# One long stretch of each matmul kind per block, with two of eight ReLUs on VectorE: a fused dynamic convolution and feed-forward kernel on one Trainium2 core

## Chip, cores, metric

The kernel runs on one core of one Trainium2 (trn2) chip. The metric is device time in microseconds (us), lower is better. All runs that are compared here are in the same (fast) state. The kernel before took 791.85 us (790.45 to 792.14).

## The reference, cut to what matters

```python
# x (8, 4096, 192), weight_gen (8, 4096, 8 heads, 7 taps), w_in (192, 2048), w_out (2048, 192)
w = softmax(weight_gen, axis=-1)                # per token and head, 7 taps
x_pad = concatenate([zeros(B, 6, D), x], axis=1)
y[b, s, h, :] = sum_k w[b, s, h, k] * x_pad[b, s + k, h, :]      # causal dynamic convolution
y = y.reshape(32768, 192)
out = maximum(y @ w_in, 0) ** 2 @ w_out         # squared-ReLU feed-forward, fp32 out
```

## The kernel before

Tokens are handled in 64 blocks of 512, eight to a batch. For each block TensorE does three things: the convolution (`yp`, as small matmuls against banded weights `bd`), MM1 (`h = y @ w_in`, 96 matmuls of 64 rows x 256 columns, twelve to each of eight "pairs" of 128-wide chunks of the 2048 hidden features) and MM2 (`o = g @ w_out`, 64 matmuls of 192 columns). Between MM1 and MM2, ScalarE takes the ReLU out of PSUM (`t`), and VectorE squares it (`g`). The softmax of the next batch is spread over the blocks: its exp is on ScalarE, the rest on VectorE. Its result goes to DRAM (`vd`) and comes back as rows (`wr`), from which VectorE makes the bands.

```python
    p_t1 = ctx.enter_context(tc.tile_pool(name="p_t1", bufs=5))
    ps_h = ctx.enter_context(tc.tile_pool(name="ps_h", bufs=3, space=bass.MemoryType.PSUM))  # 128x1024 fp32 each: yp and h
    ps_o = ctx.enter_context(tc.tile_pool(name="ps_o", bufs=1, space=bass.MemoryType.PSUM))  # 2 tiles of 128x512 fp32: o
    # ... cut ...
    def st_relu(j, fp):
        t1 = p_t1.tile([P, 2, 2, TH], f16, name="t1")
        t1_t[(j, fp)] = t1
        nc.scalar.activation(out=t1, in_=h_t[(j, fp)], func=ActF.Relu)

    def st_sq(j, fp):
        g = p_g.tile([P, 2, 2, TH], f16, name="g")
        g_t[(j, fp)] = g
        t1 = t1_t[(j, fp)]
        nc.vector.tensor_tensor(out=g, in0=t1, in1=t1, op=AluOp.mult)
    # ... cut ...
    G0, G1 = (0, 1, 2, 3), (4, 5, 6, 7)
    # ... cut: the start, until the loop over blocks ...
        for j in range(NBLK):
            # ... cut: weight_gen and x loads ...
            late = j == 2
            if j:
                if j + 1 < NBLK:
                    st_conv_alloc(j + 1)
                    st_conv(j + 1)
                    st_y_evac(j + 1)
                if not late:
                    st_bands(j + 2, 0)
            for fp in G0:
                st_mm1(j, fp)
                st_relu(j, fp)
                st_sq(j, fp)
            if j:
                for half in (0, 1):
                    st_mm2(j - 1, G1, (half,))
                    o_copy(j - 1, half, nc.scalar.copy)
                o_store(j - 1, (0, 1), nc.sync)
            # ... cut: block 0 ...
            if not late:
                st_bands(j + 2, 1)
            if hi and j:
                s = rows_of[nb]
                softmax(s, lo, hi)                 # exp on ScalarE, sum, reciprocal, scale on VectorE
                if hi == s.rh:
                    s.store(nc.sync)
            for fp in G1:
                st_mm1(j, fp)
                st_relu(j, fp)
                st_sq(j, fp)
            st_mm2(j, G0)
            # ... cut ...
            if j + 3 < NBLK:
                wr_load(j + 3)
```

MM1 and MM2 thus come in four stretches a block, of four pairs each.

The softmax here doesn't subtract the row's maximum and nothing guards it: scores larger than these inputs give would overflow.

Of the kernel before, what the change touches and what calls it, by code (L numbers as in the profile page):

```python
# [9 lines left out]
def kernel(  # L10
# [20 lines left out]
    nc = tc.nc  # L31
    f32 = mybir.dt.float32
    f16 = mybir.dt.float16
# [8 lines left out]
    P = 128  # L42
    TB = 512
    NBB = S // TB
    NBLK = B * NBB
    NF = Dff // P
    NFP = NF // 2
# [3 lines left out]
    HALO = KK - 1  # L51
    SL = 8
    TH = TB // 2
# [19 lines left out]
    p_wr = ctx.enter_context(tc.tile_pool(name="p_wr", bufs=4))  # L73
    p_bd = ctx.enter_context(tc.tile_pool(name="p_bd", bufs=3))
    p_y = ctx.enter_context(tc.tile_pool(name="p_y", bufs=2))
    p_t1 = ctx.enter_context(tc.tile_pool(name="p_t1", bufs=5))
    p_g = ctx.enter_context(tc.tile_pool(name="p_g", bufs=10))
    p_os = ctx.enter_context(tc.tile_pool(name="p_os", bufs=2))
    p_dr = ctx.enter_context(tc.tile_pool(name="p_dr", bufs=3, space=bass.MemoryType.DRAM))
# [30 lines left out]
    def load_w_in(q):  # L110
        c = slice(q * NQ, (q + 1) * NQ)
        w_sa[q] = p_st.tile([P, NQ], f32, name="w_sa")
        w_sb[q] = p_st.tile([RT, NQ], f32, name="w_sb")
        nc.sync.dma_start(out=w_sa[q], in_=moe_w_in[0:P, c])
        nc.sync.dma_start(out=w_sb[q], in_=moe_w_in[P:D, c])  # L115
# [136 lines left out]
    def x_load(j):  # L252
        x_t[j] = p_x.tile([P, NT, D], f16, name="xt")
        block_load(j, x_t[j], x[j // NBB], D, nc.gpsimd)
# [11 lines left out]
        wr = wr_t[j].rearrange("p t g c -> p t (g c)")  # L266
        block_load(j, wr, vd_t[j // NBB], H * SL, nc.sync)

    def wr_load_sbuf(j, s, order, engines):

        wr_t[j] = p_wr.tile([P, NT, HP, SL * 2], f16, name="wr")
        for n, i in enumerate(order):
            t0 = max(j * TB + tile_start(j, i), 0)
            engines[n % len(engines)].dma_start(
                out=wr_t[j][:, i].rearrange("p g c -> p (g c)"),
                in_=s.v[t0 // s.r : (t0 + P) // s.r, HALO : HALO + s.r].rearrange(
                    "p r g c e -> p r (g c e)"
                ),
            )

    def st_band(j, tiles):

# [88 lines left out]

    def st_mm2(j, fps, halves=(0, 1)):

        if fps[0] == 0:
            o_t[j] = [ps_o.tile([P, TB], f32, name=f"o{half}") for half in range(2)]
        o = o_t[j]
        for fp in fps:
            for jj in range(2):
                fc = 2 * fp + jj
                for half in halves:  # L380
                    for cc in range(2):
                        nc.tensor.matmul(  # L382
                            out=o[half][:, cc * Dm : (cc + 1) * Dm],
                            lhsT=g_t[(j, fp)][:, half, jj, cc * P : (cc + 1) * P],
                            rhs=w_o[:, fc, :],
                            start=(fc == 0 and cc == 0), stop=(fc == NF - 1),
                            skip_group_check=True,
                        )

    def st_relu(j, fp):  # L390
        t1 = p_t1.tile([P, 2, 2, TH], f16, name="t1")
        t1_t[(j, fp)] = t1
        nc.scalar.activation(out=t1, in_=h_t[(j, fp)], func=ActF.Relu)  # L393

    def st_sq(j, fp):
        g = p_g.tile([P, 2, 2, TH], f16, name="g")
        g_t[(j, fp)] = g
        t1 = t1_t[(j, fp)]
        nc.vector.tensor_tensor(out=g, in0=t1, in1=t1, op=AluOp.mult)  # L399

    def o_copy(j, half, copy):
        if half == 0:
# [17 lines left out]
            for tiles in (groups, ((NT - 1,),))[part]:  # L420
                st_band(j, tiles)

    G0, G1 = (0, 1, 2, 3), (4, 5, 6, 7)
    UNIT = 4

    with nc.allow_low_precision("fp16 matmul pipeline"), tc.manual_schedule():

        vd0 = new_vd(0)
        parts = [
            Softmax(0, P * sum(FIRST[:i]), r, v_first[i], vd0) for i, r in enumerate(FIRST)  # L430
        ]
        warm = const.tile([P, TB], f16, name="warm")
        nc.vector.memset(warm, 0.0)  # L433
        for i in (0, 1):
            nc.vector.memset(v_first[i], 0.0)

        wp = ps_h.tile([P, 2 * TB], f32, name="wp", tag="h")

        def spin(n):
            for i in range(n):  # L440
                nc.tensor.matmul(  # L441
                    out=wp[:, 0:TB], lhsT=warm[:, 0:P], rhs=warm, start=True, stop=True
                )

        def softmax(s, lo, hi):
            s.exp(lo, hi)
            s.recip(lo, hi)
            s.scale(lo, hi, nc.vector)

        vec, act, pool = nc.vector.tensor_copy, nc.scalar.copy, nc.gpsimd.tensor_copy  # L450
        s0, s1, s2 = parts
        spin(36)
        band_mask()
        s0.load(nc.sync)
        load_w_in(0)
        load_w_in(1)
        x_load_f32(0)
        s0.exp(0, s0.rh)
        s0.recip(0, s0.rh)
        s0.scale(0, s0.rh, nc.vector)  # L460
        cast_w_in(0, "straight", act)
        cast_w_in(0, "up", act)
        cast_w_in(0, "down", pool)
        cast_w_in(0, "last", act)
        cast_w_in(0, "last up", act)
        wr_load_sbuf(0, s0, (0, 1, 2, 4, 3), (nc.sync, nc.gpsimd))
        cast_w_in(1, "up", vec)
        cast_w_in(1, "down", vec)
        x_load(1)
        s1.load(nc.sync)  # L470
        for q in range(4):
            load_w_out(q, 4)
        nc.gpsimd.memset(v_first[2], 0.0)
        x_cast(0, act)
        wr_load_sbuf(1, s0, range(NT), (nc.sync,))
        s0.store(nc.sync)
        s2.load(nc.sync)
        cast_w_in(1, "straight", act)
        cast_w_in(1, "last", act)
        for i in (0, 2, 1, 3, 4):  # L480
            st_band(0, (i,))
        st_conv_alloc(0)
        st_conv(0)
        spin(4)
        s1.exp(0, s1.rh)
        st_y_evac(0)
        cast_w_in(1, "last up", act)
        x_load(2)
        nc.gpsimd.memset(v_big, 0.0)
        st_bands(1, 0)  # L490
        st_bands(1, 1)
        s1.recip(0, s1.rh)
        s1.scale(0, s1.rh, nc.vector)
        s1.store(nc.sync)
        wr_load(2)


        plan = {}

        def spread(b, rh, blocks):  # L500
            lo = 0
            for n, j in enumerate(blocks):
                left = len(blocks) - n
                hi = min(lo + -(-(rh - lo) // (UNIT * left)) * UNIT, rh)
                if lo < hi:
                    plan[j] = (b, lo, hi)
                lo = hi

        spread(0, s2.rh, (0, 1))
        for b in range(1, B):  # L510
            first = NBB * (b - 1)
            spread(b, R + HALO, range(first + (2 if b == 1 else -2), first + 5))
        rows_of = {0: s2}

        for j in range(NBLK):
            nb, lo, hi = plan.get(j, (None, 0, 0))
            after = plan.get(j + 1)
            if after and after[1] == 0:
                s = Softmax(after[0], 0, R, v_big, new_vd(after[0]))
                s.load(nc.sync)  # L520
                rows_of[after[0]] = s
            if j + 3 < NBLK:
                x_load(j + 3)

            late = j == 2
            if j:
                if j + 1 < NBLK:
                    st_conv_alloc(j + 1)
                    st_conv(j + 1)
                    st_y_evac(j + 1)  # L530
                if not late:
                    st_bands(j + 2, 0)
            for fp in G0:
                st_mm1(j, fp)
                st_relu(j, fp)
                st_sq(j, fp)
            if j:
                for half in (0, 1):
                    st_mm2(j - 1, G1, (half,))
                    o_copy(j - 1, half, nc.scalar.copy)  # L540
                o_store(j - 1, (0, 1), nc.sync)
            elif NBLK > 1:
                st_conv_alloc(1)
                st_conv(1)
                st_y_evac(1)
                st_bands(2, 0)
            if not late:
                st_bands(j + 2, 1)
            if hi and j:
                s = rows_of[nb]  # L550
                softmax(s, lo, hi)
                if hi == s.rh:
                    s.store(nc.sync)
            for fp in G1:
                st_mm1(j, fp)
                st_relu(j, fp)
                st_sq(j, fp)
            st_mm2(j, G0)
            if hi and not j:
                softmax(rows_of[nb], lo, hi)  # L560
            if late:
                st_bands(j + 2, 0)
                st_bands(j + 2, 1)
            if j + 3 < NBLK:
                wr_load(j + 3)
        st_mm2(NBLK - 1, G1, (0,))
        o_copy(NBLK - 1, 0, nc.scalar.copy)
        st_mm2(NBLK - 1, G1, (1,))
        o_store(NBLK - 1, (0,), nc.sync)
        o_copy(NBLK - 1, 1, nc.vector.tensor_copy)  # L570
        o_store(NBLK - 1, (1,), nc.scalar)
# [30 lines left out]
```

## Time and profile before

| | before |
|---|---|
| time, median of three runs | 791.85 us |
| span of the profiled execution, granted clock | 789.8 us, 0.991 |
| busy: TensorE, ScalarE, VectorE | 98%, 77%, 74% |
| share of TensorE in the chain that ended last | 94% |

The granted clock is the mean share of TensorE's full clock that the chip granted. The prediction below shows the lines; in them PE is TensorE, PEld its weight loads, DVE VectorE, ACT ScalarE, POOL GpSimd, SP SyncE, and L363 is line 363 of the kernel. A page of the profile is read here in this order: busy shares, the chain that ended last (what the end of the program hung on), the costliest groups, then the timeline of one ordinary block. One caution is needed throughout. Matmul records overlap and their ends are modelled (a 64x256 matmul is recorded with 269 ns, though the next pair starts after 109), so a wait of up to some 0.16 us between two matmuls does not appear as idle time at all. I therefore also made a **ledger**: TensorE's stream from the first MM1 on is cut into stretches of one kind; a stretch lasts from its first matmul's start to the next stretch's first; what it lasts beyond the shortest of its kind is waiting. As the shortest I take 2.726 us for 48 matmuls of MM1, 2.745 for 32 of MM2, 0.84 for a convolution, and 5.345 and 5.384 for the long stretches of MM1 and MM2.

For before the ledger is: first MM1 at 19.0 us, 753.2 us of stretches at their shortest, 13.6 us of waits, 4.0 us from the last matmul to the end.

### The profile page before, as it was taken

How to read it: one execution, taken by the hardware profiler on the slowest of the kernel's cores; microseconds unless marked ns; L12 is line 12 of the kernel's file. 1: busy time of each engine (PE TensorE's matmuls, PEld its weight loads, DVE VectorE, ACT ScalarE, POOL GpSimd, SP SyncE). 2: the span in 40 equal slices, each digit the busy share in tenths (PEclk: the TensorE clock that was granted, in tenths of full speed). 3: DMA queues.
4: the chain of work that ended last, by engine and by line, in shares of the span. 5: the costliest groups of instructions: out<-in, count | busy, mean ns of one | idle time of the engine just before them, and what ended most of it. 6: DMA issues, size and time to landing. Idle time of an engine off the chain costs nothing.

```text
span 789.8 us, 32661 instructions
## 1 busy us (share of the span) xinstructions
PE 774.0 (98%) x14888; PEld 680.1 (86%) x14888; DVE 584.0 (74%) x1042; ACT 610.7 (77%) x761; POOL 73.6 (9%) x96
## 2 busy tenths in 40 slices
PE   7889999999999999999999999999999999999997
PEld 3777888888888888888888888888888888889887
DVE  5787778777877768877777767877688777666653
ACT  6776777877887787787787787787787787787785
POOL 7101000010001000010001000011000010000000
PEclk8998999999999999999999999999999999999999
DMA  9832533336333443336333363333533344342111
GB/s 212 169 76 43 152 53 68 70 53 149 72 53 65 106 106 63 69 59 146 67 61 62 68 146 63 64 64 63 145 69 59 63 71 80 67 73 43 51 41 41
DMA packets 123929, 64.09 MB, mean 81 GB/s; under 512 B 87281, under 2 KB 121104, under 8 KB 123024
## 3 DMA queue, kind: packets, MB, share of 16 engines
q1 hardware_dynamic: 79744, 45.51, 20.8%
q0 software_dynamic: 43776, 16.31, 19.5%
q8 instruction: 116, 1.90, 1.0%
q14 instruction: 21, 0.17, 0.1%
q10 hardware_dynamic: 272, 0.20, 0.1%
HBM read 48.74 MB, written 29.36 MB: 99 GB/s over the span
## 4 chain that ended last, share of the span: by engine, by line
PE 94%; DMA 3%; DVE 2%; SPq 0%; ACT 0%; issue 0%; DVEq 0%
PE o L382 44%; PE h L363 44%; PE yp L338 7%; DMA x_st<-in_x_dram 1%; DMA wr<-v_first 1%; DVE bd L289 1%; DMA vd<-v_first 1%; DMA wr<-vd 0%; DVE g L399 0%; DVE ssum L180 0%; DVE rcp L185 0%; DVE v_big L193 0%; DVE v_first L193 0%; ACT ex L172 0%; SPq L115 0%
## 5 line engine op out<-in xcount | busy, mean ns | idle before, releaser
L393 ACT ACTIVATE t<-h 128x1024 f16<-128x1024 f32 x512 | 483.0, 1030 | 9.7 <-PE h L363 9.2
L399 DVE TENSOR_TENSOR g<-t 128x1024 f16<-128x1024 f16 x512 | 344.9, 690 | 144.5 <-ACT t L393 144.0
L363 PE MATMUL h<-y,w_i 64*128 64x256 f16 x6144 | 363.7, 271 | 0.7 <-ACT t L393 0.3
L382 PE MATMUL o<-w_o,g 128*128 128x192 f16 x4096 | 360.0, 246 | 0.0
L382 PEld LDWEIGHTS <-g 128*128 128x128 f16 x4096 | 331.5, 98 | 26.8 <-DVE g L399 16.7
L363 PEld LDWEIGHTS <-w_i 64*128 64x128 f16 x6144 | 293.0, 94 | 50.5 <-issue 12.8
L289 DVE TENSOR_TENSOR bd<-wr,mask 128x1664 f16<-128x1664 f16 (+2 forms) x201 | 160.8, 832 | 15.4 <-DMA wr<-vd 12.6
L351 ACT CAST y<-yp 128x768 f16<-128x768 f32 x64 | 51.2, 799 | 119.2 <-PE yp L338 119.2
L250 POOL DMA_DIRECT2D xt<-in_x_dram x63 | 52.2, 830 | 472.3 <-PE yp L338 448.4
L404 ACT COPY o_sb<-o 128x384 f32<-128x384 f32 x127 | 62.8, 495 | 38.2 <-PE o L382 38.2
L338 PE MATMUL yp<-bd,xt 128*32 128x104 f16 (+12 forms) x4608 | 60.4, 204 | 10.0 <-DVE bd L289 6.1
L338 PEld LDWEIGHTS <-xt 128*32 128x32 f16 (+3 forms) x4608 | 51.4, 91 | 21.1 <-issue 16.7
L180 DVE TENSOR_REDUCE ssum<-ex 128x64 f32<-128x448 f32 (+6 forms) x49 | 25.9, 529 | 32.9 <-ACT ex L172 32.9
L193 DVE TENSOR_TENSOR v_big<-ex,rcp 128x112 f16<-128x112 f32 (+3 forms) x192 | 32.8, 235 | 1.6
L172 ACT ACTIVATE ex<-wg 128x448 f32<-128x448 f32 (+6 forms) x49 | 26.5, 542 | 1.8 <-DMA wg<-in_weight_gen_dram 1.8
L185 DVE RECIPROCAL rcp<-ssum 128x64 f32<-128x64 f32 (+6 forms) x49 | 23.3, 476 | 1.7
L244 POOL DMA_DIRECT2D xt<-in_x_dram x10 | 5.7, 569 | 86.9 <-PE yp L338 86.9
L441 PE MATMUL wp<-warm 128*128 128x512 f16 x40 | 11.4, 450 | 1.3 <-DVE warm L433 1.3
L240 POOL DMA_DIRECT2D xt<-in_x_dram x7 | 3.8, 543 | 78.0 <-PE yp L338 78.0
L441 PEld LDWEIGHTS <-warm 128*128 128x128 f16 x40 | 4.3, 111 | 7.1 <-issue 2.8
L193 DVE TENSOR_TENSOR v_first<-ex,rcp 128x112 f16<-128x112 f32 (+2 forms) x32 | 6.0, 258 | 0.2
L127 ACT CAST w_i<-w_sa 128x1024 f16<-128x1024 f32 (+1 forms) x3 | 3.1, 1043 | 1.4 <-DMA w_sa<-in_moe_w_in_dram 1.4
(19 smaller groups left out, 22.9 us busy)
## 6 DMA issues: line engine op xcount, KB each, us to landing
out_dram<-o_sb SPq DMA_DIRECT2D x63, 384.0 KB, 2.8
xt<-in_x_dram POOLq DMA_DIRECT2D x46, 240.0 KB, 4.3
wg<-in_weight_gen_dram SPq DMA_DIRECT2D x6, 1064.0 KB, 5.8
wr<-vd SPq DMA_DIRECT2D x46, 80.0 KB, 3.0
vd<-v_big SPq DMA_DIRECT2D x7, 512.0 KB, 3.5
xt<-in_x_dram POOLq DMA_DIRECT2D x17, 192.0 KB, 3.9
w_sa<-in_moe_w_in_dram SPq DMA_DIRECT2D x2, 512.0 KB, 6.7
wr<-vd SPq DMA_DIRECT2D x16, 64.0 KB, 2.8
```

The costliest lines, as they stand in the source:

```text
L172: nc.scalar.activation(out=self.ex[:, lo:hi].rearrange("p r g k e -> p (r g) k e"), in_=self.wg[:, lo:hi].rearrange("p r (g e) k -> p (r g ...
L180: nc.vector.tensor_reduce(out=ssum.rearrange("p r g e -> p (r g) e"), in_=self.ex[:, lo:hi].rearrange("p r g k e -> p (r g) e k"), axis=Ax ...
L193: eng.tensor_tensor(out=bass.AP(tensor=v.tensor, offset=v.offset + lo * H * SL + lo % SL * 2 + g * SL * 2, ap=[list(v.ap[0]), [H * SL + 2, ...
L250: eng.dma_start(out=dst[:, first:last], in_=ap)
L289: nc.vector.tensor_tensor(out=bd_t[j][:, H * lo : H * hi].rearrange("p (g m c) -> p g m c", g=shape[1], c=2 * SL), in0=wr_t[j][:, i : tile ...
L338: nc.tensor.matmul(out=yp_t[j][p0 : p0 + m, col + a : col + b], lhsT=x_t[j][:, i, 32 * q : 32 * q + m], rhs=bd[:, h // 2, h % 2, a - lo : ...
L351: nc.scalar.copy(out=y, in_=yp_t[j][:, 0 : NK * TH].rearrange("p (k c) -> p k c", k=NK))
L363: nc.tensor.matmul(out=h[:, half, jj, :], lhsT=w_i[r0 : r0 + RT, slot, fc * P : (fc + 1) * P], rhs=y_t[j][r0 : r0 + RT, k, :], start=(jj = ...
L382: nc.tensor.matmul(out=o[half][:, cc * Dm : (cc + 1) * Dm], lhsT=g_t[(j, fp)][:, half, jj, cc * P : (cc + 1) * P], rhs=w_o[:, fc, :], star ...
L393: nc.scalar.activation(out=t1, in_=h_t[(j, fp)], func=ActF.Relu)
L399: nc.vector.tensor_tensor(out=g, in0=t1, in1=t1, op=AluOp.mult)
L404: copy(out=o_sb_t[j][:, half], in_=o_t[j][half][:, 0 : 2 * Dm])
```

## The change

The intent: fewer changes between matmul kinds. All eight pairs of a block go through MM1 in one stretch, then through MM2 in one. ScalarE alone could not drain eight pairs at MM1's pace (0.904 us a pair against 0.655, worked out in the prediction), so VectorE takes the ReLU of pairs 1 and 4, and ScalarE their squares. The bands of block j+2 stay ahead of MM1 in program order. The requests for the rows of block j+3 go ahead of the output store. At the start (where `spin` issues matmuls on a tile of zeros named `warm`), x is loaded ahead of the second half of `w_in`, the second softmax part later, and block 2 takes its rows from SBUF. The core of the diff, cuts marked:

```diff
-    p_t1 = ctx.enter_context(tc.tile_pool(name="p_t1", bufs=5))
+    p_t1 = ctx.enter_context(tc.tile_pool(name="p_t1", bufs=6))
+    p_t1s = ctx.enter_context(tc.tile_pool(name="p_t1s", bufs=2))
 ... cut ...
     def st_relu(j, fp):
-        t1 = p_t1.tile([P, 2, 2, TH], f16, name="t1")
+        swapped = fp in swapped_of(j)
+        t1 = (p_t1s if swapped else p_t1).tile([P, 2, 2, TH], f16, name="t1")
         t1_t[(j, fp)] = t1
-        nc.scalar.activation(out=t1, in_=h_t[(j, fp)], func=ActF.Relu)
+        if swapped:
+            nc.vector.tensor_scalar_max(out=t1, in0=h_t[(j, fp)], scalar1=0.0)
+        else:
+            nc.scalar.activation(out=t1, in_=h_t[(j, fp)], func=ActF.Relu)
 ... cut: st_sq, with ScalarE's Square for swapped pairs ...
-    G0, G1 = (0, 1, 2, 3), (4, 5, 6, 7)
+    SWAPPED = (1, 4)
+    SQ_AT = {3: (0,), 7: (2, 3, 5, 6, 7)}
+    MM2 = (0, 2, 3, 5, 6, 7, 1, 4)
 ... cut: the start ...
-        spin(36)
+        spin(42)
         load_w_in(0)
-        load_w_in(1)
         x_load_f32(0)
 ...
+        load_w_in(1)
         x_load(1)
+        wr_load_sbuf(1, [s0], range(NT), (nc.sync,))
         s1.load(nc.sync)
 ... cut: the loop ...
                 if not late:
                     st_bands(j + 2, 0)
-            for fp in G0:
+            for fp in range(NFP):
                 st_mm1(j, fp)
                 st_relu(j, fp)
-                st_sq(j, fp)
-            if j:
-                for half in (0, 1):
-                    st_mm2(j - 1, G1, (half,))
-                    o_copy(j - 1, half, nc.scalar.copy)
-                o_store(j - 1, (0, 1), nc.sync)
+                if not j:
+                    st_sq(j, fp)
+                    if fp == 1:
+                        rest_of_s1()
+                elif fp in SQ_AT:
+                    for sq in SQ_AT[fp]:
+                        st_sq(j, sq)
 ... cut ...
-            if hi and j:
+            if hi:
                 s = rows_of[nb]
                 softmax(s, lo, hi)
                 if hi == s.rh:
                     s.store(nc.sync)
-            for fp in G1: ...
-            st_mm2(j, G0)
             if j + 3 < NBLK:
                 wr_load(j + 3)
+            for fp in swapped_of(j):
+                st_sq(j, fp)
+            st_mm2(j, MM2[:4])
+            for half in (0, 1):
+                st_mm2(j, MM2[4:], (half,))
+                if more or half == 0:
+                    o_copy(j, half, nc.scalar.copy)
+            if more:
+                o_store(j, (0, 1), nc.sync)
```

## The prediction

> **What bounds the kernel now.** I read the busy shares first, then the chain that ended last, then the costliest groups. The page says:
>
> ```profile
> PE 774.0 (98%) x14888; PEld 680.1 (86%) x14888; DVE 584.0 (74%) x1042; ACT 610.7 (77%) x761; POOL 73.6 (9%) x96
> ...
> PE 94%; DMA 3%; DVE 2%; SPq 0%; ACT 0%; issue 0%; DVEq 0%
> PE o L382 44%; PE h L363 44%; PE yp L338 7%; DMA x_st<-in_x_dram 1%; DMA wr<-v_first 1%; DVE bd L289 1%; DMA vd<-v_first 1%; DMA wr<-vd 0%; DVE g L399 0%; DVE ssum L180 0%; DVE rcp L185 0%; DVE v_big L193 0%; DVE v_first L193 0%; ACT ex L172 0%; SPq L115 0%
> ```
>
> TensorE carries 94% of the chain: L382 (MM2), L363 (MM1), L338 (convolution). ScalarE and VectorE are a quarter idle, so only what changes TensorE's own stream, or makes it wait, counts. The timeline of one undisturbed block (columns: start, us, engine, line, tile, count) shows that stream:
>
> ```profile
> 406.23 0.90 PE L338 MATMUL yp<-bd,xt 128*32 128x104 f16 x72
> ...
> 407.06 2.79 PE L363 MATMUL h<-y,w_i 64*128 64x256 f16 x48
> ...
> 409.79 2.81 PE L382 MATMUL o<-w_o,g 128*128 128x192 f16 x32
> ...
> 412.53 2.90 PE L363 MATMUL h<-y,w_i 64*128 64x256 f16 x48
> ...
> 415.37 2.81 PE L382 MATMUL o<-w_o,g 128*128 128x192 f16 x32
> ...
> 418.11 0.91 PE L338 MATMUL yp<-bd,xt 128*32 128x104 f16 x72
> ```
>
> A block takes 418.11 - 406.23 = 11.88 us, in five stretches with no gap of note. The start times of single matmul records refine this: inside MM1 two matmuls start per 109 ns (54.5 each), inside MM2 one per 82.5 ns. So 48 x 54.5 = 2.62 us, yet the next stretch begins 2.73 us after this one; 32 x 82.5 = 2.64, yet 2.74 pass. **Each change of stretch costs about 0.105 us** (95 ns before the first matmul of the new kind, 10 ns after it).
>
> [...] MM1 is 64*128, MM2 128*128[...]. [...] the last output copy,
>
> ```profile
> L404 DVE COPY o_sb<-o 128x384 f32<-128x384 f32 x1 | 0.6, 558 | 2.8 <-PE o L382 2.8
> ```
>
> [...] After the early wait shown below an MM1 stretch takes 4.78 us instead of 2.79[...].
>
> **The change, part by part.**
>
> (a) Switches. Now a block has conv, MM1, MM2, MM1, MM2: five changes. Afterwards conv, MM1, MM2: three. Two fewer x 0.105 us x about 63 blocks = **-13 us**. Eighteen blocks also have an MM1 stretch of 2.83 us instead of 2.73, because ScalarE does the softmax's exp just before it (the 2.90 line above is one). That is another -2 us.
>
> (b) Work moved. Two of eight ReLUs go from ScalarE to VectorE, their squares go the other way. A VectorE ReLU on 128x1024 fp32 in PSUM is, from the 558 ns row, [...] **about 1.22 us** (estimate). In heavy blocks VectorE then does 2 x 1.22 + 6 x 0.61 + band products 1.95 + 0.55 + softmax 2.0 = 10.6 us of about 12: tight, but no bound. ScalarE keeps some 10 us (evacuation 0.80, six ReLUs 5.4, two squares about 1.9, two copies 1.0, exp 0.62).
>
> (c) New waits in MM1. This is where I differ from the intent. The rows used:
>
> ```profile
> L393 ACT ACTIVATE t<-h 128x1024 f16<-128x1024 f32 x512 | 483.0, 1030 | 9.7 <-PE h L363 9.2
> L399 DVE TENSOR_TENSOR g<-t 128x1024 f16<-128x1024 f16 x512 | 344.9, 690 | 144.5 <-ACT t L393 144.0
> L351 ACT CAST y<-yp 128x768 f16<-128x768 f32 x64 | 51.2, 799 | 119.2 <-PE yp L338 119.2
> ```
>
> TensorE fills a pair of h in 12 x 54.5 = 0.655 us. ScalarE needs 1.03 us, or 0.904 from start to start when queued. There are three h buffers. Four pairs just fit today: in single records the fourth pair starts 80 ns after its buffer's ReLU ended. Eight in a row do not. I walk it with t = 0 at the start of MM1, a ReLU startable 0.216 us after its pair's matmuls are issued, and 0.05 us from a ReLU's end to the next matmul in that buffer (both seen in single records). Buffers rotate: A = yp, h2, h5; B = h0, h3, h6; C = h1, h4, h7.
> - ReLU1 on VectorE: 1.32 + 0.216 = 1.54 to 2.76. h4 wants C at 2.63 and gets it at 2.81: **0.18 us lost**.
> - ReLU0 0.87 to 1.90; ReLU2 from 2.19; ReLU3 is queued behind it, 3.09 to 4.13. h6 wants B at 4.12, gets it at 4.18: **0.06 lost**.
> - ReLU4 on VectorE 3.68 to 4.90. h7 wants C at 4.83, gets it at 4.95: **0.12 lost**.
>
> Sum 0.36 us per block, against the 0.21 saved: **+0.15 us per block**. Even with an instant VectorE the h0-h3-h6 chain on ScalarE alone costs 4.18 - 3.94 = 0.24 us, so the switches' saving is then merely cancelled.
>
> (d) A new wait in MM2. Squares 1 and 4 stand behind the exp on ScalarE. ReLU7 ends near 7.17; exp of 0.62 to 7.67; the squares, 1.03 each as from this row's neighbour L393, end near 8.6 and 9.5. MM2 starts at 5.7 and wants pair 4, last of the first half, at 5.7 + 44 x 0.0825 = 9.35. Loss about 0.25 in blocks with the 0.62 us exp (18 of them), where (a) returned 0.1, and little in the others.
>
> The mean over a batch of eight blocks is about +0.21 us per block; x 62 = **+13 us** net, everything in (a) to (d) included.
>
> (e) The start. Before, it has three losses in the timeline:
>
> ```profile
> 13.60 0.99 ACT L262 CAST xt<-x_st 128x960 f16<-128x960 f32 x1 [3.11 <-DMA x_st<-in_x_dram]
> ...
> 30.38 2.43 DVE L289 TENSOR_TENSOR bd<-wr,mask 128x1664 f16<-128x1664 f16 x3 [4.51 <-DMA wr<-vd]
> ...
> 59.50 0.27 PE L338 MATMUL yp<-bd,xt 128*32 128x104 f16 x2 [2.74 <-DVE bd L289]
> ...
> 61.74 4.78 PE L363 MATMUL h<-y,w_i 64*128 64x256 f16 x48
> ```
>
> Fetching x before the second half of w_in takes 0.79 MB out of its way: at the 200 GB/s reached then, x lands nearer 10 us, and I give the first MM1 2 to 3 us. The rows of block 2 come from SBUF instead of by a store and reload (TensorE lost about 2.6 us there). The bands of block 4 move ahead of MM2, removing the 2.7 us wait and the slow clock after it (2.0 us). Against this: VectorE now has bands ahead of ReLU1. In block 1 those wait for rows stored late (I put some 1.7 us); in block 3 the large first softmax (1.09 + 0.95 + 1.58 in block 2) delays them by about 2 us. Also the second half of w_in, cast by GpSimd at 1.03 us a piece, may come late. Net **about -6 us**.
>
> (f) Row loads ahead of the output store only reorder two transfers that land in 3 us and are needed a block later: 0.
>
> Sum: 791.85 + 13 - 6 = about 798.
>
> **Rivals.** *The change works as meant*: no new waits, -13 -2 -6 gives 771. For it: VectorE's slack, and order lists tuned by someone with a purpose. Against: three buffers, and the 80 ns margin of today. It needs h buffers to come free earlier than any row here says. *VectorE becomes the bound*: if its ReLU takes 1.35 us, MM1 waits grow to about 0.6 us per block, and with the bands ahead of ReLU1 late in heavy blocks the time is 815 or more. For it: 10.6 us of 12, in strict order. Against: after the softmax and the next bands VectorE is free at about 12.2, and ReLU1 is wanted at 13.6. *The start alone moves*: steady waits just cancel the switches (the 0.24 us floor), giving 786 to 790.
>
> **Range and chances.** An error of 0.1 us in the steady block is 6 us, and the start is uncertain by 4. So 780 to 813. Faster than 776 needs nearly every wait of (c) absent: 0.09. Slower than 807.7 needs 0.15 us per block more than worked out, or a bad start: 0.17. Within 2%: 0.74.
>
> **What would show it.** Changes of stretch near 0.105 us, three per block: (a). VectorE's ReLU row near 1220 ns: (b). "PE h" waiting for t of VectorE at the fifth and eighth pair, for t of ScalarE at the seventh, 0.3 to 0.4 us per block: (c). MM2 waiting for ScalarE's g in blocks with the long exp: (d). First MM1 near 16 to 17 us, no loss near 59 us, a wait for VectorE in blocks 1 and 3: (e). A steady block near 11.93 us without exp and 12.2 with the long one. The prediction is wrong if MM1 of a steady block runs in 5.34 us without waits, or if VectorE is late for ReLU1 in every block.

## The result, and the profile after

The changed kernel took **826.24 us** (median of 4 runs, 824.39 to 827.1); before, in the same rounds, 792.0 us. The ratio is 1.043 (95% interval 1.0403 to 1.0457). The change made the kernel 4.3% slower, outside the predicted range of 780 to 813 us.

The page of the changed kernel, its busy shares and the chain that ended last:

```profile
PE 788.7 (96%) x14894; PEld 704.2 (85%) x14894; DVE 624.9 (76%) x1040; ACT 631.5 (77%) x759; POOL 78.3 (9%) x100
...
PE 67%; ACT 10%; DVE 10%; DMA 6%; issue 4%; SPq 2%; ACTq 0%; DVEq 0%
```

The busy shares hardly tell anything: 96 instead of 98%. The chain does: TensorE carried 94% of it, and now 67%; ScalarE, VectorE and DMA have entered it. The costliest groups on the two drain engines (count, busy us, mean ns of one, idle before):

```profile
L407 ACT ACTIVATE t<-h 128x1024 f16<-128x1024 f32 x386 | 374.3, 1023 | 52.4 <-PE h L369 52.4
...
L405 DVE TENSOR_SCALAR t<-h 128x1024 f16<-128x1024 f32 x126 | 154.3, 1224 | 143.6 <-PE h L369 140.0
...
L295 DVE TENSOR_TENSOR bd<-wr,mask 128x1664 f16<-128x1664 f16 (+2 forms) x201 | 160.8, 837 | 41.4 <-DMA wr<-vd 31.2
...
L414 ACT ACTIVATE g<-t 128x1024 f16<-128x1024 f16 x126 | 126.8, 1067 | 0.0
```

VectorE's ReLU takes 1224 ns, close to the estimate of 1.22 us, which can be worked out from the trace of before: 558 ns for 384 elements a partition (the output copy), and 640 more at 1.04 ns each (its softmax sums, `ssum`, take 967 ns for 784 elements and 386 for 224). The new fact is in the third line: the bands waited 31.2 us for rows. Now the timeline of an ordinary block with the long exp, to be held against the one in the prediction:

```profile
406.36 5.85 PE L369 MATMUL h<-y,w_i 64*128 64x256 f16 x96
...
407.29 1.02 ACT L407 ACTIVATE t<-h 128x1024 f16<-128x1024 f32 x1
407.96 1.23 DVE L405 TENSOR_SCALAR t<-h 128x1024 f16<-128x1024 f32 x1 [3.22 <-PE h L369]
...
410.11 1.22 DVE L405 TENSOR_SCALAR t<-h 128x1024 f16<-128x1024 f32 x1 [0.32 <-PE h L369]
...
412.15 5.74 PE L388 MATMUL o<-w_o,g 128*128 128x192 f16 x64
413.49 0.64 ACT L173 ACTIVATE ex<-wg 128x448 f32<-128x448 f32 x1
414.00 2.01 ACT L414 ACTIVATE g<-t 128x1024 f16<-128x1024 f16 x2
...
416.07 1.60 PEld L388 LDWEIGHTS <-g 128*128 128x128 f16 x20 [0.34 <-ACT g L414]
...
417.82 0.91 PE L344 MATMUL yp<-bd,xt 128*32 128x104 f16 x72
```

MM1 lasts 412.15 - 406.36 = 5.79 us, where 96 matmuls at 54.5 ns and one change of kind need 5.35. MM2 lasts 5.67 us where 5.38 would do: its last pairs wait for ScalarE's squares, which stand behind the exp. The block takes 12.30 us, against 11.88 before.

The start, from the same timeline:

```profile
15.67 2.14 PE L369 MATMUL h<-y,w_i 64*128 64x256 f16 x36
...
23.07 0.93 ACT L173 ACTIVATE ex<-wg 128x784 f32<-128x784 f32 x1 [5.62 <-DMA wg<-in_weight_gen_dram]
23.91 4.86 ACT L407 ACTIVATE t<-h 128x1024 f16<-128x1024 f32 x5
...
24.96 5.46 PE L369 MATMUL h<-y,w_i 64*128 64x256 f16 x60 [7.15 <-ACT t L407]
```

MM1 does start 3.4 us sooner, fills its three buffers, and then stands 7.15 us: ReLU0 is behind an exp on ScalarE whose input lands only at 23.1 us. And one block at the edge of a batch (the block whose rows two blocks on are requested behind a store):

```profile
93.01 2.84 PE L369 MATMUL h<-y,w_i 64*128 64x256 f16 x48
...
97.06 1.96 DVE L295 TENSOR_TENSOR bd<-wr,mask 128x1664 f16<-128x1664 f16 x2 [5.41 <-DMA wr<-vd]
98.94 1.22 DVE L405 TENSOR_SCALAR t<-h 128x1024 f16<-128x1024 f32 x1
...
100.21 4.46 PE L369 MATMUL h<-y,w_i 64*128 64x256 f16 x48 [4.36 <-DVE t L405]
```

VectorE waits for rows, then makes bands for the block after next, and only then takes ReLU1. TensorE stands because ReLU1 holds one of three h buffers.

The two ledgers, in us:

| | before | after | difference |
|---|---|---|---|
| until the first MM1 | 19.0 | 15.7 | -3.4 |
| stretches at their shortest | 753.2 | 739.6 | -13.6 |
| waits in MM1 of block 0 | 1.7 | 9.3 | +7.6 |
| waits in the other MM1 | 5.1 | 48.0 | +42.9 |
| waits in MM2 | 4.6 | 8.7 | +4.1 |
| waits in the convolution | 2.2 | 0.2 | -2.0 |
| after the last matmul | 4.0 | 3.6 | -0.3 |
| span | 789.8 | 825.2 | +35.4 |

So the switches were saved as intended, 13.6 us of them, and 52.6 us of new waits came. The 48.0 us split in two: 63 blocks x 0.44 us = 27.7 us in every MM1, and 20.3 us in eleven MM1 stretches of 6.1 to 11.6 us (blocks 1, 3 and 5, six later batch edges, and blocks 22 and 46).

### The profile page after: what moved, and what is told of

Its sections match the earlier page's. It is cut to its first block, busy times and chain, and to the rows that moved or that the text cites. A ratio compares the mean times of both kernels' runs of the same rounds, so it can differ in the third digit from the quotient of the medians.

```text
span 825.2 us, 32633 instructions
## 1 busy us (share of the span) xinstructions
PE 788.7 (96%) x14894; PEld 704.2 (85%) x14894; DVE 624.9 (76%) x1040; ACT 631.5 (77%) x759; POOL 78.3 (9%) x100
## 3 DMA queue, kind: packets, MB, share of 16 engines
q0 software_dynamic: 43776, 16.31, 18.9%
## 4 chain that ended last, share of the span: by engine, by line
PE 67%; ACT 10%; DVE 10%; DMA 6%; issue 4%; SPq 2%; ACTq 0%; DVEq 0%
PE h L369 35%; PE o L388 27%; PE yp L344 5%; ACT g L414 5%; ACT t L407 4%; DMA wr<-vd 4%; DVE g L416 3%; DVE t L405 2%; DVE bd L295 2%; ACT ex L173 1%; DMA wg<-in_weight_gen_dram 1%; SPq L279 1%; DVE v_big L194 1%; DVE rcp L186 1%; DVE ssum L181 1%
## 5 line engine op out<-in xcount | busy, mean ns | idle before, releaser
L407 ACT ACTIVATE t<-h 128x1024 f16<-128x1024 f32 x386 | 374.3, 1023 | 52.4 <-PE h L369 52.4
L369 PE MATMUL h<-y,w_i 64*128 64x256 f16 x6144 | 376.3, 272 | 27.5 <-DVE t L405 18.1
L369 PEld LDWEIGHTS <-w_i 64*128 64x128 f16 x6144 | 316.6, 95 | 73.6 <-issue 52.4
L388 PE MATMUL o<-w_o,g 128*128 128x192 f16 x4096 | 354.4, 246 | 3.3 <-ACT g L414 1.2
L405 DVE TENSOR_SCALAR t<-h 128x1024 f16<-128x1024 f32 x126 | 154.3, 1224 | 143.6 <-PE h L369 140.0
L416 DVE TENSOR_TENSOR g<-t 128x1024 f16<-128x1024 f16 x386 | 243.3, 685 | 1.7 <-ACT t L407 1.7
L295 DVE TENSOR_TENSOR bd<-wr,mask 128x1664 f16<-128x1664 f16 (+2 forms) x201 | 160.8, 837 | 41.4 <-DMA wr<-vd 31.2
L421 ACT COPY o_sb<-o 128x384 f32<-128x384 f32 x127 | 61.0, 480 | 96.8 <-PE o L388 96.8
L414 ACT ACTIVATE g<-t 128x1024 f16<-128x1024 f16 x126 | 126.8, 1067 | 0.0
L344 PEld LDWEIGHTS <-xt 128*32 128x32 f16 (+3 forms) x4608 | 50.3, 91 | 11.6 <-issue 11.4
L344 PE MATMUL yp<-bd,xt 128*32 128x104 f16 (+11 forms) x4608 | 58.9, 202 | 0.8 <-DVE bd L295 0.7
```

The source lines that it names most:

```text
L295: nc.vector.tensor_tensor(out=bd_t[j][:, H * lo : H * hi].rearrange("p (g m c) -> p g m c", g=shape[1], c=2 * SL), in0=wr_t[j][:, i : tile ...
L344: nc.tensor.matmul(out=yp_t[j][p0 : p0 + m, col + a : col + b], lhsT=x_t[j][:, i, 32 * q : 32 * q + m], rhs=bd[:, h // 2, h % 2, a - lo : ...
L369: nc.tensor.matmul(out=h[:, half, jj, :], lhsT=w_i[r0 : r0 + RT, slot, fc * P : (fc + 1) * P], rhs=y_t[j][r0 : r0 + RT, k, :], start=(jj = ...
L388: nc.tensor.matmul(out=o[half][:, cc * Dm : (cc + 1) * Dm], lhsT=g_t[(j, fp)][:, half, jj, cc * P : (cc + 1) * P], rhs=w_o[:, fc, :], star ...
L405: nc.vector.tensor_scalar_max(out=t1, in0=h_t[(j, fp)], scalar1=0.0)
L414: nc.scalar.activation(out=g, in_=t1, func=ActF.Square)
```

## The experiments

The theory after the result: four separate causes, each a wait of TensorE. (i) Three rotating h buffers are too few for eight pairs in a row (27.7 us). (ii) Bands stand ahead of ReLU1 on VectorE (20.3 us). (iii) The exp stands ahead of the two squares on ScalarE (most of 8.7 us). (iv) The start. The rivals: VectorE and ScalarE simply have too much work; or a long stretch is slow in itself; or the start's reordering is good and the loop spoils it. All kernels gave correct results.

### Four buffers instead of three: two steps

In the changed kernel PSUM holds three h buffers of 128x1024 fp32 and two output tiles of 128x512. The fourth buffer takes the place of the two outputs; whether there is room for one beside them, no run tests. With one long MM1 that is possible: no output accumulates while MM1 runs. (In the kernel before it was not: an output lived across an MM1 stretch.)

```diff
-    ps_h = ... tc.tile_pool(name="ps_h", bufs=3, space=PSUM)
-    ps_o = ... tc.tile_pool(name="ps_o", bufs=1, space=PSUM)
+    ps_h = ... tc.tile_pool(name="ps_h", bufs=4, space=PSUM)
-            o_t[j] = [ps_o.tile([P, TB], f32, name=f"o{half}") for half in range(2)]
+            o_t[j] = ps_h.tile([P, 2, TB], f32, name="o", tag="h")
 ... cut: MM2 and the copies address the one tile ...
```

> The changed kernel with one thing different: the two output accumulators take a turn in the same rotation as the h buffers, so that four double banks rotate instead of three and MM1 of a block can use the one that MM2 does not need yet. Theory (three buffers are what MM1 waits for, 0.446 us in each steady block): the MM1 stretch of a steady block falls from 5.79 to about 5.34 us, a block without exp from 12.01 to 11.57 us. MM2 then starts earlier against the same ScalarE order, so its wait for the squares behind a long exp grows from 0.29 to about 0.5 us. Total about 800 us (797 to 806). Rival (the two drain engines are simply too slow, or a long MM1 stretch is slow in itself): the stretch stays at 5.6 us or more and the total at 815 us or more.

Measured: 839.75 us, ratio to before 1.0585 (1.056 to 1.061). In total a miss by 40 us, yet MM1 did what the theory said. Its timeline:

```profile
406.18 1.48 PE L387 MATMUL o<-w_o,g 128*128 128x192 f16 x16 [0.57 <-ACT o_sb L420]
...
407.59 0.91 PE L343 MATMUL yp<-bd,xt 128*32 128x104 f16 x72
...
408.44 5.41 PE L368 MATMUL h<-y,w_i 64*128 64x256 f16 x96
...
413.78 3.80 PE L387 MATMUL o<-w_o,g 128*128 128x192 f16 x44
```

MM1 is 413.78 - 408.44 = 5.34 us; the steady wait is gone. But MM2 has a wait that I put in myself: both halves of the output were now one tile, so the second half waited 0.57 us for the copy of the first. With everything around it that made each MM2 at least 6.11 us, 0.73 more than the shortest, 46 us in 63 blocks. The second step copies both halves in one instruction after MM2:

```diff
             for half in (0, 1):
                 st_mm2(j, MM2[4:], (half,))
-                if more or half == 0:
-                    o_copy(j, half, nc.scalar.copy)
+            if more:
+                o_sb_t[j] = p_os.tile([P, 2, 2 * Dm], f32, name="o_sb")
+                nc.scalar.copy(out=o_sb_t[j], in_=o_t[j][:, :, 0 : 2 * Dm])
 ... cut: the last block ...
```

> Four rotating double banks as in the first experiment, which made the second half of MM2 wait 0.57 us for the copy of the first half, because both halves were then one tile; here both halves are copied in one instruction after MM2, so that this wait, which the experiment itself had added, is gone. Theory: MM1 stays at 5.35 us, the shortest MM2 returns from 6.11 to 5.38 us, only the wait for ScalarE's squares stays in it (0.3 to 0.5 us in blocks with exp); total about 795 us (789 to 802), 30 us under the changed kernel. Rival (four buffers only move the wait from MM1 into MM2, whatever the copies do): the MM2 stretch stays at 5.9 us or more and the total at 815 us or more.

Measured: 803.55 us, ratio 1.0121 (1.0093 to 1.015); a little over the stated 802. Ledger: waits in the other MM1 48.0 -> 15.8 us, with 5.35 us in 53 of 63 stretches; MM2 8.7 -> 17.8 us, since MM1 now ends earlier against the same ScalarE order. Net 22.7 us. Cause (i) is shown: the waits follow the number of buffers, with the same work on every engine but for one merged copy. The rival of a slow long stretch falls: a stretch of 96 runs at the pace of two of 48.

### Which pairs VectorE drains

```diff
-    SWAPPED = (1, 4)
-    SQ_AT = {3: (0,), 7: (2, 3, 5, 6, 7)}
-    MM2 = (0, 2, 3, 5, 6, 7, 1, 4)
+    SWAPPED = (2, 5)
+    SQ_AT = {3: (0, 1), 7: (3, 4, 6, 7)}
+    MM2 = (0, 1, 3, 4, 6, 7, 2, 5)
```

> The changed kernel with pairs 2 and 5 drained by VectorE instead of 1 and 4, and the orders of squares and MM2 to match. Theory (a buffer is free 1.02 us after ScalarE and 1.23 us after VectorE begins, three buffers rotate): walked with the durations of the changed kernel's trace, the wait in a steady MM1 falls from 0.45 to about 0.28 us, its stretch from 5.79 to 5.62 us, and a ReLU wanted 0.65 us later on VectorE shortens the long MM1 stretches by as much; total about 811 us (806 to 817). Rival (the waits of MM1 do not follow from which pair an engine drains): 5.79 us stays and the total is 823 us or more.

Measured: 813.46 us, ratio 1.0273 (1.0231 to 1.0315). The steady MM1 is 5.65 us, 0.30 over the shortest, where the walk of the buffers gave 0.28. This is the same mechanism read the other way: same number of buffers, same engines, other turns.

### Bands after the squares

```diff
-                if not late:
-                    st_bands(j + 2, 0)
 ...
-            if late:
+            if j:
                 st_bands(j + 2, 0)
             st_bands(j + 2, 1)
```

> The changed kernel with the band products of block j+2 issued after the squares of block j in every block, not ahead of its first ReLU on VectorE. Theory (VectorE stands at a band product that waits for a DMA or for a late softmax, and ReLU1 behind it holds an h buffer): the eleven long MM1 stretches (6.1 to 11.6 us) after block 0 fall to 5.79 us, 20 us in all, total about 806 us (803 to 810). Rival (VectorE has too much work there in any order): the loss comes back as waits of the convolution for bands, and the total stays above 816 us.

Measured: 807.38 us, ratio 1.0182 (1.0163 to 1.0201). Every MM1 after block 0 but one is 5.71 to 5.79 us, the longest 6.14; its waits fall from 48.0 to 28.0 us, which is 63 x 0.44. Block 5, which stood 4.36 us in the lines above:

```profile
88.20 5.85 PE L369 MATMUL h<-y,w_i 64*128 64x256 f16 x96
...
89.79 1.23 DVE L405 TENSOR_SCALAR t<-h 128x1024 f16<-128x1024 f32 x1 [1.09 <-PE h L369]
...
93.98 5.45 PE L388 MATMUL o<-w_o,g 128*128 128x192 f16 x64
...
96.09 2.42 DVE L295 TENSOR_TENSOR bd<-wr,mask 128x1664 f16<-128x1664 f16 x3
```

Cause (ii) is shown with its size, 20 us. The rival (too much work for VectorE in any order) falls: the same work in another order costs TensorE nothing beyond the steady wait.

### Why the rows were late at the batch edges

In every eighth block the store of the new softmax precedes the request for rows in SyncE's queue. Experiment: the request first (from block 2 on; before that the rows depend on the store).

```diff
+            if j > 1 and j + 3 < NBLK:
+                wr_load(j + 3)
             if hi:
                 s = rows_of[nb]
                 softmax(s, lo, hi)
                 if hi == s.rh:
                     s.store(nc.sync)
-            if j + 3 < NBLK:
+            if j <= 1:
                 wr_load(j + 3)
```

> The changed kernel with the request for the rows of block j+3 put ahead of the softmax and its store in the DMA queue of SyncE, from block 2 on. Theory (in every eighth block the rows are requested only after a store that waits for VectorE's last softmax piece, so they land late, the bands wait for them, and ReLU1 waits behind the bands): the seven MM1 stretches of 6.9 to 7.2 us at the batch edges fall to 5.79 us, and the one of 11.6 us in block 5 falls by several us; total about 814 us (811 to 818). Rival (the rows are late because the DMA engines are busy, not because of their place in the queue): the edges stay at 6.9 us or more and the total at 822 us or more.

Measured: 815.16 us, ratio 1.0242 (1.0207 to 1.0278). The stretch of 11.6 us in block 5 and the six at the edges (6.9 to 7.1 us) fall to 5.78 or 5.79 us, but for one (block 29) that keeps 6.13; waits in the other MM1 fall from 48.0 to 36.7 us. So the place in the queue is the cause there. Blocks 1 and 3 keep theirs (4.3 and 1.9 us, the steady part included). Block 46, the seventh that I had counted as an edge, is not one: its wait grew from 1.8 to 3.5 us. In its case the first request for rows sits in SyncE's queue for more than 5 us, right behind the load of the last batch's weights; why it sits there is open.

### Squares ahead of the exp

```diff
+            for fp in swapped_of(j):
+                st_sq(j, fp)
             if hi:
                 s = rows_of[nb]
                 softmax(s, lo, hi)
 ...
-            for fp in swapped_of(j):
-                st_sq(j, fp)
             st_mm2(j, MM2[:4])
```

> The changed kernel with ScalarE's two squares ahead of the softmax's exp instead of behind it. Theory: every MM2 stretch becomes 5.38 us (now 5.67 in blocks with a 0.62 us exp, 5.46 with a 0.41 us exp), 8.6 us less in all, total about 818 us; the exp and the softmax on VectorE come some 2 us later, which may give 1 or 2 us back where the bands and ReLU1 queue behind them. Rival (the MM2 wait has another cause, such as the squares of VectorE): the MM2 stretches keep their lengths and the total stays at 825 us or more.

Measured: 839.78 us, ratio 1.0575 (1.0517 to 1.0632): 22 us over the expectation. MM2 did lose its waits, 8.7 -> 0.5 us. The waits in the other MM1 grew from 48.0 to 68.1 us. The view of waits says where they sit:

```profile
DVE ssum L181 <- ACT ex L173: 52.9, 47, 2.4
DVE bd L295 <- DMA wr<-vd: 33.4, 9, 6.3
PE h L369 <- DVE t L405: 29.5, 10, 5.8
```

The softmax comes about 2 us later on VectorE (first line: it waits 52.9 us for the exp, and 2.6 us in the changed kernel), and with it the store, the rows, the bands and ReLU1. The granted clock was 0.973 in this run, below the 0.991 of the changed kernel. Each digit of the page's PEclk line is the granted clock, in tenths, in a 40th of the span (the changed kernel first, then this run):

```profile
PEclk9899999999999999999999999999999999999999
...
PEclk9899999999999999999899999999899999999999
```

In detail the trace has, after 60 us, seven stretches of 3.4 or 6.8 us at half clock, each at one of the longer waits for ReLU1, where the changed kernel has one. Half of TensorE's busy time in them is 14.2 us, against 1.7 us in the changed kernel. So by this estimate some 12 of the 22 us are the clock's. So (iii) is real, but mending it alone feeds (ii), more than I had allowed for.

### The start

First, the exp of the second softmax part behind ReLU1, so that ReLU0 need not wait for its input:

```diff
-        s1.exp(0, s1.rh)
         nc.gpsimd.memset(v_first[2], 0.0)
 ...
         def rest_of_s1():
+            s1.exp(0, s1.rh)
+            s1.recip(0, s1.rh)
```

> The changed kernel with the exp of the second softmax part of the first block set behind ReLU1 on ScalarE instead of ahead of ReLU0. Theory (ScalarE waits for that exp's input, which the reordered loads bring at 23.1 us, and ReLU0 behind it holds an h buffer for 7 us): TensorE's wait of 7.15 us goes, but the next wait stands just behind it, for the second half of w_in that GpSimd casts until 22.5 us, so only about 3 us come back: total about 823 us. Rival (the exp alone is in the way): the whole 7 us come back, total about 819 us.

Measured: 825.36 us, ratio 1.0408 (1.0384 to 1.0431); within the spread of the changed kernel's 826.24. The 3 us that were expected did not come back, and so neither did the rival's 7. The timeline shows three waits in the place of one:

```profile
19.68 1.31 PE L369 MATMUL h<-y,w_i 64*128 64x256 f16 x16 [1.88 <-ACT t L407]
...
23.15 0.73 PE L369 MATMUL h<-y,w_i 64*128 64x256 f16 x7 [1.50 <-POOL w_i L128]
...
25.54 4.02 PE L369 MATMUL h<-y,w_i 64*128 64x256 f16 x36 [1.66 <-ACT t L407]
```

After the first comes the cast of the second half of `w_in`, as expected, and then the exp again, which now holds ReLU2. Second, the four corners of start and loop. The old start under the changed loop, and the new start under the old loop (both mechanical, the text between the warming matmuls and the loop is exchanged, with the calls that belong to it):

> The changed kernel with the order of the first loads, casts and the second softmax part as in the kernel before (36 warming matmuls, second half of w_in ahead of x, rows of block 2 by a store and a reload); the loop as changed. Theory: first MM1 near 19 us instead of 15.7, but the MM1 of block 0 falls from 14.7 to about 8 us, so conv of block 1 starts some 3 us earlier than now, and the rows of block 3 come earlier, which shortens the long MM1 of block 1 (9.9 us); total about 818 us (812 to 822). Rival (the reordered loads are a gain and the loss of the start is the loop's alone): the total is 826 us or more.

> The kernel before with the reordered start of the changed kernel and its own loop: the fourth corner, beside before (792.6), changed (826.2) and changed loop with the old start (822.5). Theory (the new start wins 3.4 us on the first MM1 and loses more in block 0, where ReLU0 stands behind an exp whose input comes late): 794 us (791 to 798). Rival (the new start is good and only the changed loop cannot use it): 788 us or less.

| ratio to before | old start | new start |
|---|---|---|
| old loop | 1 | 0.9992 (0.9962 to 1.0022), 795.12 us |
| changed loop | 1.0371 (1.0347 to 1.0394), 822.52 us | 1.043 (1.0403 to 1.0457), 826.24 us |

The new start is worth nothing with the old loop and costs about half a per cent with the changed one. Most of the loss is the loop's. (The old start's result lies half a microsecond over the stated 822.)

### All the mends together

Four buffers with one copy, bands after the squares, squares ahead of the exp; the new start as in the changed kernel.

> The kernel of the run above with the band products after the squares on VectorE, and ScalarE's two squares ahead of the exp. Theory (the four causes, buffers, bands, exp ahead of squares, and the start, add up): steady MM1 5.35, MM2 5.38 to 5.45 us, a block 11.57 us in all kinds of block, against 11.78 and 11.88 before; total about 772 us (766 to 780), some 2.5% under the kernel before. Rival (with all waits of TensorE gone VectorE or ScalarE is the bound in blocks with a softmax): such blocks stay at 11.8 us or more and the total is 785 us or more.

Measured: **771.03 us**, ratio 0.9723 (0.9705 to 0.9742). Its timeline in blocks with the long exp:

```profile
384.01 0.91 PE L343 MATMUL yp<-bd,xt 128*32 128x104 f16 x72
...
384.86 5.41 PE L368 MATMUL h<-y,w_i 64*128 64x256 f16 x96
...
390.20 5.45 PE L387 MATMUL o<-w_o,g 128*128 128x192 f16 x64
...
395.58 0.91 PE L343 MATMUL yp<-bd,xt 128*32 128x104 f16 x72
```

The block takes 395.58 - 384.01 = 11.57 us. The ledger of the loop: 0.6 us of waits in the other MM1, 0.05 in MM2. What separately gave 22.7 us (buffers), 18.9 us (bands) and -13.5 us (squares first) gives 55 us together, because each mend had left a wait for the next. The rival, too much work for VectorE or ScalarE, has no room left: they do the work of the changed kernel in blocks 0.7 us shorter.

What is left lies at the start. Two attempts on top of this kernel: loads reordered again (softmax input earlier, `w_out` after the casts), and the old start.

```diff
         load_w_in(1)
         x_load(1)
+        s1.load(nc.sync)
         wr_load_sbuf(1, [s0], range(NT), (nc.sync,))
-        s1.load(nc.sync)
-        for q in range(4):
-            load_w_out(q, 4)
 ... exp behind ReLU1 as above ...
         cast_w_in(1, "last up", pool)
+        for q in range(4):
+            load_w_out(q, 4)
```

> The mended loop (771.0 us) with the start mended as well: weight_gen of the second softmax part is loaded ahead of the rows of block 1, its exp stands behind ReLU1 on ScalarE, and the 1.6 MB of w_out are requested only after GpSimd has cast the second half of w_in. Theory (the 6.3 us wait in the MM1 of block 0 comes from the order in which those loads share the DMA engines): MM1 of block 0 falls from 13.2 to some 9 us, some of it comes back as a wait of the first MM2 for w_out or of the conv of block 2 for its rows; total about 767 us (764 to 770). Rival (the start is bound by the sum of the bytes, whatever their order): the total stays at 770 us or more.

Measured: 771.22 us (ratio 0.9702, 0.9671 to 0.9733; before was slower in these rounds, 796.15 us). Nothing clear of the noise was gained (the mended loop's ratio, 0.9723, lies inside this interval): the waits of block 0's MM1 fell from 7.9 to 5.5 us, and 2.4 us came back in the first MM2, which the profile shows waiting for `g` (the last of `w_out` landed at 30.0 us, 3.3 us after that MM2 began). That fits the rival, that the start is bound by the sum of what must be loaded, but the next run speaks against it: with another order it does gain.

> The mended loop (four buffers, one output copy, bands after the squares, squares ahead of the exp) with the start of the kernel before. Theory: with the changed loop the old start reached the MM1 of block 1 at 35.0 us, the new one at 37.4; the mended loop with the new start reaches it at 37.1, so about 2 us come back: total about 769 us (766 to 772). Rival (the two starts are equal): 771 us or more.

Measured: **768.26 us**, ratio 0.9668 (0.9634 to 0.9702). This is the best version, 3.3% under the kernel before, and 3.0 us under the previous one on the same chip, so the order of the start (loads, and which engine casts) does matter. Of the gain over the mended loop with the new start, 2.8 us, the ledger shows 7.4 us less waiting in the first MM1 against a later first MM1, by 1.0 us, and more waits in the first MM2 and convolutions. In this run the first MM1 came at 16.6 us, and at 18.3 and 19.0 in the other runs of this start. ScalarE began to cast x at 12.1 us here, at 13.1 and 13.6 there; why x landed sooner is open.

## Why the prediction was wrong, point by point

| step | predicted, us | measured, us | by |
|---|---|---|---|
| (a) changes of kind | -13 | -13.6 | ledger; block of 11.57 in the mended loop |
| (b) VectorE's ReLU | 1.22 each | 1.224 | group of the page |
| (c) waits for h buffers in each MM1 | 0.36 x 62 = +22 | 0.44 x 63 = +27.7 | bands experiment leaves 28.0 |
| (d) MM2 behind the exp | about +4.5 | +8.7 | ledger; 0.5 with the squares first |
| (e) first MM1 | -2 to -3 | -3.4 | timeline |
| (e) bands ahead of ReLU1 | +3.7, blocks 1 and 3 | +20.3, eleven blocks | bands experiment |
| (e) wait in block 0 | named, no number | 9.3, 1.7 before | ledger |
| (a) and (e) other waits of before that go | -2 and about -7 | -11.9 | ledger |

**Right.** Steps (a) and (b), and the mechanism of (c) and (d): the change pays for the saved switches with waits for PSUM buffers and for squares. The sizes were low. For (c), the walk had waits at pairs 4, 6 and 7 of 0.18, 0.06 and 0.12 us. In a steady block of the trace they are at pairs 3, 4 and 7, of 0.03, 0.22 and 0.19. ReLU0 and ReLU1 each began 0.06 us later than walked (0.93 for 0.87, 1.60 for 1.54), and all else followed from that; why they did is open. For (d), the short exp of 0.41 us also cost 0.08 us a block, and the early, longer ones up to 0.7. Together (c) and (d) account for about 10 of the 28 us by which the prediction missed.

**Wrong.** The step that failed is **(e)**, "Net about -6 us": by the ledger its parts come to about +15 us (-3.4 for the first MM1, +7.6 of waits in block 0, +20.3 for the bands, less about 10 of early waits that went). Two things were missed in it.
- "VectorE now has bands ahead of ReLU1" was seen, and priced for blocks 1 and 3 alone. It costs in every block where rows come late, and I had walked only an undisturbed block. In the kernel before, late bands (a wait of 2.79 us for rows ahead of 90.42 us) delayed squares that MM2 needed much later; in the changed one they delay a ReLU that holds one of three h buffers, so bands now have to be done within the 1.6 us from MM1's start to ReLU1. Block 5 and the six later batch edges were there to be found in the program: a store that waits for the softmax stands ahead of the rows in the queue. Step (f) looked at the output store alone.
- In block 0, the prediction named the second half of `w_in` as a risk. The first wait was another, an exp ahead of ReLU0 whose input had been moved back behind other loads; `w_in` was the second, shown when the exp was moved.

The rival "VectorE becomes the bound" had the right side of the range (815 or more) and half of the cause. It too named bands that are late ahead of ReLU1, but in a VectorE short of time, with ReLUs of 1.35 us (measured 1.224); the bands experiment shows that VectorE's order was at fault. The rival "works as meant" (771 us) is what the mended loop reached, at 771.03 us, once a fourth buffer, a merged copy and two changes of order made it so. That the figures meet is partly luck: the rival had 6 us from the new start, which was worth nothing with the old loop and cost with the changed one.

On the clock: it was halved after the early wait of before (granted clock 0.5 from 59.0 to 65.9 us), in which TensorE was idle for 2.74 us; the last section has what the traces show.

**Open:** why the rows of block 48 are requested late (the wait in block 46); how short the start can be made by a better order of loads.

## What to carry to other kernels

Before making a stretch longer, walk its output buffers with the drain durations of the trace: the saving per switch is small (0.1 us here), and one buffer too few cost more than two switches (0.44 us a block against 0.21). VectorE took its work in program order here (in block 5 ReLU1 began at 98.94 us, behind bands that had waited 5.41 us for rows). When such an engine is given work that frees a scarce buffer, everything ahead of that work in its queue becomes critical, and so do the DMAs that this work waits for; put whatever may wait behind it. Walk the unusual blocks (first ones, batch edges) as well as the ordinary one, and judge the mends of such waits together, since each alone hands its gain to the next.

## What the traces show of the hardware

- A change between 64*128 and 128*128 stretches cost 0.105 us, and two fewer per block took 0.21 us off (11.78 to 11.57 us in blocks without a long exp).
- VectorE, from fp32 in PSUM: the ReLU of 1024 elements a partition took 1224 ns and the copy of 384 took 558, so 666 ns more for 640 more elements. ScalarE, for 1024 elements a partition: 1067 ns for the square, from SBUF, and 1023 for the ReLU, from PSUM.
- The turnaround of a PSUM buffer: a ReLU began 0.04 us after the modelled end of its last matmul (before, 407.93 us), and the next matmul into a buffer 0.05 us after the ReLU's end (after, 408.37 us).
- The granted clock: in the traces of before and after it fell to half five times ahead of the last matmul (at 14.6 and 59.0 us; at 22.3, 42.8 and 100.8 us), for 3.41 or 6.83 us each, and its changes lie whole multiples of 3.41 us apart. In the 3.41 us ahead of the five falls TensorE's records filled 0, 34, 0, 26 and 18%. Cut on the same grid, the other 455 windows at full clock, from the first matmul to the last of both traces, were filled to 49% or more.
